# Another written order for the prologue and chunk 0 of fused attention and FFN, with the first loads in the list and a few stages on VectorE

## The chip, the cores and the metric

One core of one Trainium2 chip runs the kernel. The metric is the device time of one launch in microseconds (us). Before the change the median of three runs is 906.14 us (904.85 to 907.07).

## The reference

For each of 8 batches and 8 heads, q, k, v are 576 x 64. Heads 0 to 3 use a local mask (a row sees itself and the 31 rows before it), heads 4 to 7 a strided one (a row sees earlier rows with the same index modulo 32).

```python
scores = np.where(mask, (q @ k.T) / 8.0, -1e9)
attn = np.exp(scores - scores.max(-1)); attn /= attn.sum(-1) + 1e-9
x = concat_heads(attn @ v)                       # 8 x 576 x 512
xn = (x - mu) / np.sqrt(var + 1e-6) * g_ln       # over the 512 columns
out = x + np.maximum(xn @ w_ch1, 0) @ w_ch2      # 512 -> 2048 -> 512
```

The two weight matrices arrive as 64-bit floats, and the kernel turns them into 32-bit ones itself.

## The kernel before, in words

**Tiling.** Attention works on pairs of heads: pair k = 0, 1, 2, 3 is batch 0 (0 and 2 strided, 1 and 3 local), 4 to 7 batch 1, and so on to 31. The FFN works on 9 chunks of 512 rows, chunk c being batch c's first 512 rows (the ninth takes what is left of all batches). The FFN's hidden width of 2048 is cut into 16 steps f of 128. Every matmul of the FFN is split into a high part (`fp32r`) and a rest, so a step is 8 + 4 matmuls for the first layer and 12 for the second.

**Two programs.** Chunks 1 to 8 run in a loop over c and f; the change leaves it as it is. What comes before, the prologue (pairs 0 to 3, whose result is chunk 0's x) and chunk 0 itself (with the weights' conversion and pairs 4 to 8 between), is issued in the order of a hand-written string, `ORDER`. Each engine runs its instructions strictly in that order, and waits by semaphore for what it reads or overwrites. There is no planner at run time: `one(op, k, i, buf)` (L842) carries out one word `op:k:i:buf` of the string.

**The words**, with engine and what they do for pair k:
- `T:k:i` PE, 24 small matmuls that transpose the rows of q (i=0) or k (i=1); `c` ACT, copies that out of PSUM.
- `S` PE, the scores (48 or 80 matmuls); `mask`, `max` DVE; `sub` POOL, minus the row maximum; `exp` ACT.
- `PP` PE, transposes the probabilities; `pt` ACT, copies them; `V` PE, times v; `den`, `xo` DVE, divides by the row sum.
- `X` PE, transposes the result; `xh` ACT and `xl` DVE, its high part and rest, which the first layer reads; `st` stores the result.
- `r`, `v` SP, loads of q and k (8 DMAs) and v for later pairs; `vs` POOL, a shifted copy of v; `tp` DVE, transposes `r`'s tile.

For weight step f: `W` SP, two loads of 512 KB (`w_load`, L221); `sc` ACT, `low` DVE or `lowA` ACT, `mg` and `sg` DVE, which assemble 32-bit floats (i=0 first layer, i=1 second); `byg` POOL, times g; `add` POOL, two adds; `cm` PE, the column mean; `cen` DVE, subtracts it; `hi` ACT and `lo` POOL, high part and rest. Then `F` and `H` PE, the first layer with the high part and the rest (8 and 4 matmuls; for step 0 the last pair's 2 come as `Fb`), `hh` ACT and `hl` DVE after the ReLU, `G` PE, the second layer (12 matmuls).

**What sets the order around the change.** `buf` picks one of three PSUM rooms (`ps_a`, `ps_o[0]`, `ps_o[1]`); a new tile there waits until the old one has been read. The two `ps_o` rooms become the second layer's accumulators at `G:0`. `sc` has a single PSUM buffer (`ps_r`), freed by `sg`. Before `ORDER` starts, lines 802 to 815 issue all loads of batch 0: pair 0's q and k as halves on the SP and ACT queues, q of pairs 1 to 3 on SP's, k on ACT's, then g, then v of the four pairs, all on SP. The first `W` of the list comes behind them on the same queue:

```python
for p in first:
    p.load_v(once=True)
```

Of the kernel before, what the change touches and what calls it, by code (L numbers as in the profile page):

```python
# [32 lines left out]
add:4 hh:2 sg:4:1 st:4 hl:2 sc:5:0 X:4::0 lo:3:0 F:3 mg:5:0 xh:4 r:6 lo:3:1 lowA:5:1 xl:4 H:3
sg:5:0 cm:4::0 hh:3 G:2 cen:4 byg:5 sc:5:1 hl:3 lowA:6:1 v:5 add:5 mg:5:1 hi:4:0 sg:5:1 lowA:6:0
lo:4:0 F:4 max:5 sc:6:0 lowA:7:0 mg:6:0 sub:5 lowA:7:1 cm:5::0 sg:6:0 H:4 cen:5 W:8 sc:6:1 byg:6
G:3 hh:4 mg:6:1 add:6 hi:4:1 hl:4 hi:5:0 sg:6:1 lo:5:0 cm:6::0 sc:7:0 F:5 cen:6 W:9 exp:5 lo:4:1
mg:7:0 hi:5:1 sg:7:0 H:5 tp:6 byg:7 sc:7:1 PP:5::0 lowA:8:0 G:4 add:7 st:0 hh:5 hi:6:0 hl:5 lo:5:1
pt:5 r:7 mg:7:1 hi:6:1 S:6::0 lo:6:0 sg:7:1 lowA:9:0 lowA:8:1 F:6 mask:6 sc:8:0 max:6 cm:7::0
mg:8:0 sg:8:0 sub:6 H:6 st:3 G:5 hh:6 cen:7 byg:8 st:2 hl:6 hi:7:0 lo:6:1 tp:7 sc:8:1 hi:7:1
V:5::0 add:8 lowA:9:1 r:8 F:7 mg:8:1 sg:8:1 lo:7:0 den:5 sc:9:0 xo:5 H:7 mg:9:0 sg:9:0 cm:8::0  # L40
hh:7 G:6 exp:6 byg:9 hl:7 W:10 sc:9:1 cen:8 add:9 mg:9:1 hi:8:0 PP:6::0 hi:8:1 sg:9:1 lo:8:0 F:8
tp:8 pt:6 W:11 lo:7:1 hi:9:1 cm:9::0 H:8 lo:8:1 sc:10:0 cen:9 lowA:10:0 G:7 lowA:10:1 mg:10:0 W:12
hi:9:0 sg:10:0 hh:8 byg:10 sc:10:1 hl:8 S:8::0 lowA:11:0 lo:9:0 mg:10:1 F:9 lowA:11:1 sg:10:1 v:6
add:10 mask:8 sc:11:0 H:9 mg:11:0 lo:9:1 lowA:12:1 sg:11:0 cm:10::0 G:8 hh:9 cen:10 byg:11 W:13
sc:11:1 hi:10:0 mg:11:1 hi:10:1 lo:10:0 hl:9 lowA:12:0 S:7::0 sg:11:1 add:11 sc:12:0 F:10 mask:7
W:14 lo:10:1 mg:12:0 cm:11::0 sg:12:0 H:10 max:7 sc:12:1 byg:12 G:9 hh:10 cen:11 st:5 add:12
mg:12:1 hi:11:0 hl:10 lowA:13:1 W:15 lo:11:0 sg:12:1 hi:11:1 cm:12::0 F:11 max:8 sc:13:0 lowA:13:0
cen:12 H:11 mg:13:0 hi:12:0 v:7 sg:13:0 lo:12:0 X:5::0 hh:11 G:10 xh:5 lo:11:1 sc:13:1 xl:5
lowA:14:1 hl:11 sub:7 hi:12:1 mg:13:1 V:6::0 lowA:14:0 r:9 byg:13 F:12 sg:13:1 den:6 add:13 xo:6
sc:14:0 H:12 lo:12:1 lowA:15:0 mg:14:0 exp:7 cm:13::0 sg:14:0 G:11 hi:13:1 cen:13 byg:14 xr:0  # L50
hh:12 sc:14:1 hl:12 lo:13:1 hi:13:0 mg:14:1 X:6::0 lo:13:0 sg:14:1 F:13 xh:6 add:14 xr:1 sc:15:0
xl:6 H:13 sub:8 mg:15:0 cm:14::0 hh:13 G:12 cen:14 xr:2 sg:15:0 hi:14:0 hl:13 byg:15 xs:0 PP:7::0
lo:14:0 F:14 pt:7 tp:9 st:6 lowA:15:1 add:15 sc:15:1 H:14 r:10 cm:15::0 hh:14 G:13 cen:15 exp:8
hl:14 hi:14:1 mg:15:1 hi:15:0 sg:15:1 lo:15:0 V:7::0 hi:15:1 xr:3 F:15 lo:15:1 den:7 xo:7 lo:14:1
xs:2 X:7::0 v:8 H:15 G:14 hh:15 xh:7 hl:15 xl:7 v:9 tp:10 PP:8::0 pt:8 xs:3 st:7 r:11 xs:1
# [9 lines left out]
def kernel(  # L65
# [737 lines left out]
    for p in first:  # L803
        if p.k in BY_DVE:
            p.load_qk(early.tile([P, 2 * S], F32, name=f"raw{p.id}"))
        elif p.k == 0:
            for i in range(2):
                p.load_rows(i, nc.sync, slice(0, 1))
                p.load_rows(i, nc.scalar, slice(1, 2))
        else:  # L810
            p.load_rows(0, nc.sync)
            p.load_rows(1, nc.scalar)
    nc.sync.dma_start(gcol, g_ln.rearrange("(c p) -> p c", p=P))
    for p in first:
        p.load_v(once=True)

# [211 lines left out]
```

## Time and profile before

| | |
|---|---|
| median of 3 runs | 906.14 us (904.85 to 907.07) |
| the profiled execution | span 907.3 us from the first to the last instruction; the page gives no other time for it |
| PE, matmuls | 884.9 us busy, 98% of the span, 7606 matmuls |
| DVE, ACT, POOL busy | 435.4, 199.7, 147.9 us |
| mean granted TensorE clock | 0.992 |
| F:1, the first layer's second step, starts | at 54.70 us |
| chunk 1 starts (F of its step 0 at 152.55 us, its first G at 162.74 us) | chunks 1 to 8 fill the rest |

The times of the rows are microseconds from the first instruction. A busy time counts an engine's instructions, not its waits. The idle time in brackets behind a row is what the engine spent waiting right before that instruction, and whose end released it; "issue" is a wait for nothing that the profile shows. On PE a row is a run of matmuls; PEld are the weight loads that go with them, one for each. SPq and ACTq are the instructions that issue DMAs.

### The profile page before, as it was taken

How to read it: one execution, taken by the hardware profiler on the slowest of the kernel's cores; microseconds unless marked ns; L12 is line 12 of the kernel's file. 1: busy time of each engine (PE TensorE's matmuls, PEld its weight loads, DVE VectorE, ACT ScalarE, POOL GpSimd, SP SyncE). 2: the span in 40 equal slices, each digit the busy share in tenths (PEclk: the TensorE clock that was granted, in tenths of full speed). 3: DMA queues.
4: the chain of work that ended last, by engine and by line, in shares of the span. 5: the costliest groups of instructions: out<-in, count | busy, mean ns of one | idle time of the engine just before them, and what ended most of it. 6: DMA issues, size and time to landing. Idle time of an engine off the chain costs nothing.

```text
span 907.3 us, 18531 instructions
## 1 busy us (share of the span) xinstructions
PE 884.9 (98%) x7606; PEld 728.8 (80%) x7606; DVE 435.4 (48%) x864; ACT 199.7 (22%) x326; POOL 147.9 (16%) x186
## 2 busy tenths in 40 slices
...
GB/s 166 226 257 179 247 196 114 147 111 119 134 142 109 102 137 120 124 91 141 109 134 93 135 104 141 100 127 124 116 85 91 49 128 0 1 1 93 0 1 47
DMA packets 339621, 102.98 MB, mean 114 GB/s; under 512 B 276944, under 2 KB 331344, under 8 KB 339536
## 3 DMA queue, kind: packets, MB, share of 16 engines
...
q8 instruction: 60, 0.98, 0.5%
q14 instruction: 25, 0.20, 0.1%
...
## 4 chain that ended last, share of the span: by engine, by line
PE 93%; DMA 2%; DVE 1%; issue 1%; SPq 1%; POOL 1%; ACT 0%; DVEq 0%; POOLq 0%; ACTq 0%
PE po L775 42%; PE ph L748 28%; PE ph L755 14%; PE m L515 2%; PE m L445 2%; DMA s<-in_moe_w_ch_dram 1%; PE t L371 1%; PE s L445 1%; DMA rows<-in_q_dram 1%; PE av L515 1%; SPq L351 1%; PE cm L281 1%; PE px L636 0%; PE pp L501 0%; POOL r L270 0%
## 5 line engine op out<-in xcount | busy, mean ns | idle before, releaser
L775 PE MATMUL po<-w,hh 128*128 128x512 f32 x1152 | 359.2, 393 | 0.0
L765 DVE SCALAR_TENSOR_TENSOR hl<-ph,hh 128x512 fp32r<-128x512 f32 x144 | 99.3, 690 | 367.0 <-ACT hh L760 367.0
L775 PEld LDWEIGHTS po<-w,hh 128*128 128x128 f32 x1152 | 213.4, 188 | 44.8
L748 PE MATMUL ph<-xh,w 128*128 128x512 f32 x576 | 226.0, 392 | 1.4 <-ACT w L294 1.2
L775 PE MATMUL po<-w,hl 128*128 128x512 f32 x576 | 224.5, 390 | 0.0
L748 PE MATMUL ph<-xl,w 128*128 128x512 f32 x576 | 224.5, 390 | 0.0
L760 ACT ACTIVATE hh<-ph 128x512 fp32r<-128x512 f32 x144 | 86.1, 598 | 483.7 <-PE ph L755 469.0
L755 PE MATMUL ph<-xh,w 128*128 128x512 f32 x576 | 155.3, 392 | 0.0
L748 PEld LDWEIGHTS ph<-xh,w 128*128 128x128 f32 x576 | 108.3, 188 | 24.1 <-ACT w L294 1.4
L775 PEld LDWEIGHTS po<-w,hl 128*128 128x128 f32 x576 | 108.1, 188 | 23.1
L755 PEld LDWEIGHTS ph<-xh,w 128*128 128x128 f32 x576 | 108.2, 189 | 22.5 <-POOL w L298 0.2
L748 PEld LDWEIGHTS ph<-xl,w 128*128 128x128 f32 x576 | 108.3, 188 | 22.0
L491 POOL TENSOR_TENSOR sm<-sm,mx 128x648 f32<-128x648 f32 (+1 forms) x32 | 40.6, 1269 | 440.4 <-DVE mx L486 440.4
L723 POOL TENSOR_TENSOR rs<-rs,mhalf 128x1 f32<-128x1 f32 x36 | 19.7, 548 | 286.5 <-DVE rs L722 286.5
L497 ACT ACTIVATE sm<-sm 128x648 f32<-128x648 f32 (+1 forms) x32 | 23.8, 742 | 104.3 <-POOL sm L491 104.3
L298 POOL TENSOR_TENSOR w<-r,w 128x512 fp32r<-128x512 f32 x32 | 41.1, 1297 | 7.3 <-ACT w L294 6.9
L687 DVE TENSOR_TENSOR xl<-xo,xh 128x512 fp32r<-128x512 f32 x24 | 16.6, 692 | 38.8 <-ACT xh L686 38.8
L686 ACT ACTIVATE xh<-xo 128x512 fp32r<-128x512 f32 x24 | 15.2, 632 | 62.0 <-DMA pd<-sm 18.2
L486 DVE TENSOR_REDUCE mx<-sm 128x12 f32<-128x648 f32 (+1 forms) x32 | 26.3, 822 | 2.1
L565 DVE TENSOR_TENSOR xo<-m,den 64x64 f32<-64x64 f32 (+3 forms) x120 | 27.1, 289 | 0.0
L781 DVE SCALAR_TENSOR_TENSOR x<-po,rs,x 128x512 f32<-128x512 f32 x36 | 24.5, 737 | 2.0 <-PE po L775 1.8
L718 DVE BATCH_NORM_STATS2 st<-x 128x6 f32<-128x512 f32 x36 | 24.3, 674 | 0.0
...
## 6 DMA issues: line engine op xcount, KB each, us to landing
...
```

The source lines that it names most:

```text
L298: nc.gpsimd.tensor_tensor(out=t[:, 1], in0=self.w[i], in1=t[:, 0].bitcast(F32), op=ALU.subtract)
L445: nc.tensor.matmul(o, lhsT, rhs, start=True, stop=True, tile_position=(64 * h, pos))
L486: nc.vector.reduce_max(mx[:, :, 0:nt], sm, axis=AX.X)
L491: nc.gpsimd.tensor_tensor(out=sm, in0=sm, in1=mx[:, :, 0:nt].unsqueeze(3).broadcast_to([P, 2, nt, sm.shape[3]]), op=ALU.subtract)
L515: nc.tensor.matmul(at(h, t)[m * j:m * (j + 1)], self.p_cols(rows, t, j), self.v[rows, n, 0:w], start=True, stop=True, tile_position=(64 * ...
L565: nc.vector.tensor_tensor(out=xo[r, t0:t1, h0:h1].rearrange("p t h d -> p h t d"), in0=av, in1=den[r, h0:h1, t0:t1].unsqueeze(3).broadcast_to(
L748: nc.tensor.matmul(ph, w1h[:, cc], x[:, cc, :], start=(new and n == 0 and i == 0), stop=False)
L755: nc.tensor.matmul(ph, w1l[:, cc], xt[c][0][:, cc, :], start=False, stop=(cc == NCC - 1))
L760: nc.scalar.activation(out=hh, in_=ph, func=AF.Relu)
L765: nc.vector.scalar_tensor_tensor(out=hl, in0=ph, scalar=0.0, in1=hh.bitcast(F32), op0=ALU.max, op1=ALU.subtract)
L775: nc.tensor.matmul(po[i], hx[:, cs], w, start=(f == 0 and n == 0), stop=(f == NFC - 1 and n == 2))
L781: nc.vector.scalar_tensor_tensor(out=x, in0=po[i], scalar=rs, in1=x, op0=ALU.mult, op1=ALU.add)
```

## The change

The loads of batch 0 become words of the list: `R:k:i` loads the rows of q or k, `g` loads g, and `v:0` to `v:3` load v. All of k but pair 0's second half and pair 1 now goes on SP's queue. `W:0` stands ahead of `R:2:0` and all `v`; `r:4` ahead of `v:1`, and `W:1` behind `v:1`. The list is another one throughout: both are given here up to `G:0`. A word that ends in `D` runs its stage on DVE (`subD:0`, `bygD:14`, `addD:14`, `loD:13:0`, `addD:15`, `loD:15:0`, all POOL before). Step 1's `low` goes to ACT (`lowA:1:0`, `lowA:1:1`), `low:7:1` and `low:15:0` to DVE. The parameters `eng` and `copy` are handed down for that, `BY_DVE` and `ONCE` go, and 2 is written as `CC`; the arithmetic stays.

```diff
 ORDER = """
-T:0:0:0 T:0:1:1 c:0:0: c:0:1: T:1:0:2 S:0::0 c:1:0: T:1:1:2 mask:0 max:0 T:2:1:0 c:1:1: sub:0
-S:1::1 c:2:1: exp:0 T:2:0:2 mask:1 max:1 PP:0::0 c:2:0: T:3:0:1 sub:1 pt:0 c:3:0: V:0::2 exp:1
-vs:1 S:2::0 den:0 xo:0 PP:1::1 mask:2 X:0::2 pt:1 max:2 W:0 T:3:1:0 xh:0 sub:2 V:1::1 xl:0 c:3:1:
-S:3::2 den:1 r:4 xo:1 low:0:0 sc:0:0 low:0:1 exp:2 mg:0:0 mask:3 PP:2::1 X:1::0 pt:2 sg:0:0 W:1
-max:3 xh:1 V:2::2 sc:0:1 xl:1 sub:3 tp:4 byg:0 exp:3 W:2 PP:3::0 add:0 den:2 S:4::1 pt:3 mg:0:1
-vs:3 xo:2 cm:0::0 low:1:0 X:2::2 W:3 mask:4 sg:0:1 V:3::1 xh:2 max:4 sc:1:0 cen:0 sub:4 xl:2 r:5
-hi:0:0 lowA:2:0 mg:1:0 hi:0:1 lo:0:0 F:0 exp:4 den:3 sg:1:0 lowA:3:0 lo:0:1 xo:3 sc:1:1 low:1:1
-byg:1 X:3::1 mg:1:1 v:4 sg:1:1 add:1 PP:4::2 xh:3 sc:2:0 xl:3 cm:1::0 mg:2:0 Fb:0 pt:4 lowA:3:1
-W:4 cen:1 H:0 lowA:2:1 sg:2:0 hi:1:0 tp:5 byg:2 V:4::0 hh:0 sc:2:1 add:2 hl:0 S:5::1 hi:1:1 st:1
-mg:2:1 lo:1:0 cm:2::2 sg:2:1 F:1 W:5 mask:5 sc:3:0 lo:1:1 hi:2:1 cen:2 H:1 mg:3:0 hi:2:0 G:0
...
+R:0:0 T:0:0:1 c:0:0: R:0:1 R:1:1 T:0:1:0 T:1:1:1 c:0:1: c:1:1: S:0::0 R:1:0 R:2:1 mask:0 T:1:0:1
+c:1:0: T:2:1:0 max:0 W:0 subD:0 sc:0:0 exp:0 S:1::1 low:0:0 c:2:1: PP:0::2 mg:0:0 sg:0:0 mask:1
+R:2:0 T:2:0:0 pt:0 v:0 R:3:0 V:0::2 max:1 sc:0:1 low:0:1 g:0 mg:0:1 sub:1 den:0 xo:0 sg:0:1 c:2:0:
+S:2::0 X:0::2 mask:2 exp:1 byg:0 add:0 R:3:1 hi:0:1 lo:0:1 T:3:1:1 xh:0 c:3:1: r:4 T:3:0:0 max:2 v:1
+c:3:0: xl:0 sub:2 exp:2 cm:0::1 cen:0 hi:0:0 PP:1::2 tp:4 S:3::1 pt:1 mask:3 lo:0:0 max:3 W:1
+lowA:1:0 PP:2::2 vs:1 S:4::1 sc:1:0 sub:3 pt:2 v:3 mg:1:0 vs:3 lowA:1:1 mask:4 sg:1:0 V:1::0 exp:3
+PP:3::2 sc:1:1 max:4 v:2 W:2 byg:1 den:1 mg:1:1 pt:3 V:2::1 sub:4 lowA:2:0 r:5 xo:1 X:1::2 den:2
+xh:1 add:1 sg:1:1 W:3 sc:2:0 hi:1:1 xo:2 xl:1 V:3::0 den:3 v:4 X:2::1 lo:1:1 cm:1::2 xh:2 lowA:2:1
+mg:2:0 xo:3 sg:2:0 X:3::0 sc:2:1 byg:2 xl:2 W:4 F:0 cen:1 exp:4 mg:2:1 xh:3 hi:1:0 add:2 cm:2::2
+xl:3 PP:4::1 lowA:3:0 W:7 sg:2:1 tp:5 sc:3:0 lowA:3:1 lo:1:0 Fb:0 H:0 S:5::0 pt:4 mg:3:0 sg:3:0 hh:0
+st:2 hl:0 V:4::1 hi:2:1 cen:2 sc:3:1 byg:3 add:3 mg:3:1 den:4 F:1 W:5 cm:3::2 W:6 hi:2:0 lowA:4:0
+lowA:4:1 lo:2:0 mask:5 xo:4 W:8 lowA:7:0 H:1 cen:3 sg:3:1 hh:1 sc:4:0 X:4::0 hi:3:0 low:7:1 lo:2:1
+hl:1 mg:4:0 sg:4:0 xh:4 G:0 sc:4:1 F:2 H:2 lo:3:0 max:5 hi:3:1 byg:4 mg:4:1 G:1 sg:4:1 lowA:5:0
...
 """
...
     def one(op, k, i, buf):
         p = pairs[k]
-        if op == "T":
+        eng, copy = nc.gpsimd, nc.scalar.copy
+        if op.endswith("D"):
+            op, eng, copy = op[0:-1], nc.vector, nc.vector.tensor_copy
+        if op == "R":
+            if k == 0:
+                p.load_rows(i, nc.sync, slice(0, 1))
+                p.load_rows(i, nc.scalar, slice(1, 2))
+            else:
+                p.load_rows(i, nc.scalar if k == 1 and i == 1 else nc.sync)
+        elif op == "g":
+            nc.sync.dma_start(gcol, g_ln.rearrange("(c p) -> p c", p=P))
+        elif op == "T":
...
         elif op == "v":
-            p.load_v(once=ONCE)
+            p.load_v(once=p.b == 0)
```

## Rows read from the trace of the kernel before

**Rows 1.** Busy time by stage: PE, PEld, DVE, ACT, POOL; granted clock, DMA share, GB/s
```profile
23.44:44.27 20.83, 12.88 (x430) 10.79 (x421) 17.33 (x30) 9.47 (x17) 8.17 (x8) 0.92 0.89 233
44.27:54.70 10.43, 8.22 (x154) 6.28 (x155) 9.46 (x18) 8.07 (x14) 7.87 (x10) 0.84 0.77 212
54.70:112.62 57.92, 57.70 (x503) 47.00 (x503) 49.17 (x77) 40.41 (x70) 45.17 (x47) 1.00 0.83 226
112.62:160.02 47.40, 47.35 (x448) 38.31 (x449) 35.66 (x68) 22.13 (x39) 28.34 (x32) 1.00 0.73 155
160.02:907.30 747.28, 741.18 (x5701) 610.59 (x5699) 318.60 (x652) 110.01 (x178) 46.42 (x55) 1.00 0.50 96
```
**Rows 2.** Timeline of PE up to F:1: start, length, line, count [idle before, releaser]
```profile
8.28 1.21 PE L371 MATMUL t<-ident,rows 96*64 96x96 f32 x24 [1.68 <-DMA rows<-in_q_dram]
...
12.52 0.68 PE L445 MATMUL s<-kt_l,qt_l 64*32 64x64 f32 x42
16.28 0.88 PE L445 MATMUL s<-kt_l,qt_l 64*32 64x64 f32 x38 [3.09 <-issue]
17.09 2.19 PE L371 MATMUL t<-ident,rows 96*64 96x96 f32 x24
19.21 1.54 PE L501 MATMUL pp<-ident,sm 128*128 128x128 f32 x6
20.68 1.71 PE L371 MATMUL t<-ident,rows 96*64 96x96 f32 x24
22.32 0.93 PE L515 MATMUL av<-v_s,pt 54*64 54x65 f32 x48
...
28.65 0.76 PE L515 MATMUL av<-v_l,pt 64*32 64x65 f32 x52 [1.27 <-issue]
...
33.03 0.31 PE L445 MATMUL s<-kt_l,qt_l 64*32 64x64 f32 x5 [2.83 <-issue]
...
49.43 0.79 PE L281 MATMUL cm<-bsum,mean 128*128 128x128 f32 x2 [1.24 <-POOL bsum L277]
...
52.63 0.93 PE L515 MATMUL av<-v_s,pt 54*64 54x65 f32 x48
53.49 1.04 PE L445 MATMUL s<-kt_l,qt_l 64*32 64x64 f32 x80
...
54.70 0.47 PE L748 MATMUL ph<-xh,w 128*128 128x512 f32 x1
```
**Rows 3.** DVE's groups between 23.44 and 54.70 us: busy, mean ns, idle before
```profile
L258 DVE SCALAR_TENSOR_TENSOR p<-p,s 128x512 uint32<-128x512 uint32 x6 | 4.1, 688 | 0.2
L264 DVE SCALAR_TENSOR_TENSOR r<-s,p 128x512 uint32<-128x512 uint32 x5 | 3.3, 657 | 0.0
...
L254 DVE TENSOR_SCALAR s<-s 128x512 uint32<-128x512 uint32 x4 | 1.9, 497 | 0.0
...
L565 DVE TENSOR_TENSOR xo<-av,den 128x768 f32<-128x768 f32 x2 | 1.9, 950 | 0.0
...
L473 DVE TENSOR_TENSOR sm<-s,mask_s 128x648 f32<-128x648 f32 x2 | 1.6, 821 | 0.0
...
L765 DVE SCALAR_TENSOR_TENSOR hl<-ph,hh 128x512 fp32r<-128x512 f32 x1 | 0.7, 693 | 0.5 <-ACT hh L760 0.5
```
**Rows 4.** Timeline of DVE, POOL and ACT: pair 0's max, sub, exp, step 0's sc
```profile
11.35 0.83 DVE L486 TENSOR_REDUCE mx<-sm 128x12 f32<-128x648 f32 x1
12.34 1.27 POOL L491 TENSOR_TENSOR sm<-sm,mx 128x648 f32<-128x648 f32 x1 [3.43 <-DVE mx L486]
13.71 0.76 ACT L497 ACTIVATE sm<-sm 128x648 f32<-128x648 f32 x1
...
27.64 0.64 ACT L244 ACTIVATE p<-s 128x512 f32<-128x512 f32 x1
```
**Rows 5.** Busy time in stretches of 2 us, columns as in rows 1
```profile
0.00:2.00 2.00, 0.95 (x4) 0.95 (x5) 0.96 (x11) 0.00 (x0) 1.26 (x10) 1.00 0.07 16
...
10.00:12.00 2.00, 2.00 (x62) 1.86 (x56) 1.48 (x2) 0.65 (x2) 0.00 (x0) 1.00 1.24 213
...
14.00:16.00 2.00, 0.00 (x0) 0.00 (x0) 0.00 (x0) 0.47 (x1) 0.00 (x0) 0.73 0.37 72
...
34.00:36.00 2.00, 1.49 (x54) 1.22 (x52) 1.93 (x5) 1.77 (x3) 0.20 (x1) 1.00 1.04 379
```
**Rows 6.** Timeline of SP's queue: loads of W:0 (first half) and r:4
```profile
20.22 0.49 SPq L224 DMA_DIRECT2D s<-in_moe_w_ch_dram  x1
...
21.39 3.04 SPq L351 DMA_DIRECT2D raw<-in_q_dram  x4
24.47 4.30 SPq L351 DMA_DIRECT2D raw<-in_k_dram  x4
```
**Rows 7.** The page's DMA queues: PE's instructions, packets and MB
```profile
q8 instruction: 60, 0.98, 0.5%
```

More of the change, by code (lines that the diff above doesn't have):

```diff
@@ L33 @@
[L33 to L55, printed above, removed]
-"""
-BY_DVE = ()
@@ new lines @@
+lowA:4:1 lo:2:0 mask:5 xo:4 W:8 lowA:7:0 H:1 cen:3 sg:3:1 hh:1 sc:4:0 X:4::0 hi:3:0 low:7:1 lo:2:1
+hl:1 mg:4:0 sg:4:0 xh:4 G:0 sc:4:1 F:2 H:2 lo:3:0 max:5 hi:3:1 byg:4 mg:4:1 G:1 sg:4:1 lowA:5:0
+lowA:5:1 sc:5:0 xl:4 mg:5:0 hi:4:1 hh:2 add:4 sg:5:0 hl:2 cm:4::0 lo:3:1 sub:5 lowA:6:0 F:3 sc:6:0
+mg:6:0 byg:5 sg:6:0 lowA:6:1 st:1 add:5 st:3 exp:5 cen:4 sc:5:1 cm:5::0 H:3 byg:6 mg:5:1 add:6
+sg:5:1 cen:5 hi:4:0 lowA:8:0 sc:7:0 hh:3 hi:5:1 mg:7:0 sg:7:0 G:2 sc:7:1 hl:3 r:6 cm:6::0 mg:7:1
+lo:4:0 lowA:8:1 sg:7:1 hi:5:0 cen:6 F:4 H:4 sc:8:0 mg:8:0 lo:4:1 hi:6:0 sg:8:0 hh:4 sc:6:1 PP:5::0
@@ new lines @@
+tp:6 mg:6:1 pt:5 G:3 hi:7:1 hl:4 S:6::0 sg:6:1 sc:8:1 hi:6:1 W:9 mask:6 F:5 lo:5:1 v:5 lo:5:0 byg:7
+mg:8:1 lowA:9:0 lowA:9:1 st:0 sg:8:1 lo:6:0 r:7 byg:8 sc:9:0 add:7 cm:7::0 H:5 cen:7 lo:7:1 hh:5
+hi:7:0 max:6 hl:5 mg:9:0 lo:6:1 sub:6 G:4 st:4 add:8 sg:9:0 tp:7 V:5::0 hi:8:1 W:10 exp:6 sc:9:1
+lo:8:1 den:5 xo:5 mg:9:1 F:6 byg:9 sg:9:1 lowA:10:0 cm:8::0 lo:7:0 H:6 sc:10:0 cen:8 mg:10:0
+lowA:10:1 sg:10:0 hi:8:0 hh:6 G:5 hl:6 r:8 W:11 sc:10:1 add:9 byg:10 W:12 PP:6::0 W:14 mg:10:1 W:13
+sg:10:1 st:5 lo:8:0 tp:8 hi:9:1 F:7 pt:6 cm:9::0 hi:10:1 H:7 sc:11:0 cen:9 lowA:11:0 mg:11:0 G:6
```

83 lines of the change are left out of this document (39 added, 44 removed).

## The prediction

> **What bounds the kernel now.** I read the busy time by stage first, then PE's timeline, and then asked what DVE, POOL and SP did where PE stood idle. From F:1 at 54.70 us on, PE is the bound: in the 57.92 us to 112.62 it is busy 57.70, in the next 47.40 it is busy 47.35, and the eight loop chunks behind run at 741.18 of 747.28, which the change leaves alone [rows 1]. An order can't make that part shorter, it can only bring holes into it. So what there is to win lies ahead of F:1. There PE waits: 1.68 us for pair 1's rows, 3.09 us inside pair 1's scores, 1.27 and 2.83 us in V:1 and S:3, 1.24 us for step 1's column sum [rows 2].
>
> Second reading: from den:0, which DVE starts as V:0 ends, to F:1 are 31.3 us (23.44 to 54.70), and in them DVE is busy 17.33 + 9.46 = 26.8 [rows 1]. DVE has no long holes there but 4.5 us of short ones, ACT is at 17.5 and POOL at 16.0. So F:1 comes when DVE has done its list from den:0 on, plus what DVE waits for PE. Both lists have done the same PE work by F:1 (all T, S:0 to 5, PP:0 to 4, V:0 to 4, X:0 to 3, cm:0 to 2, F, Fb and H of step 0), so PE itself saves nothing: the change can only start DVE's list earlier, shorten it, or remove waits.
>
> **Part 1: up to den:0.** The new list opens T:0:0 T:0:1 T:1:1 S:0 T:1:0 T:2:1 S:1. These are the same matmuls that stand before the 3.09 us hole now, in another order: 12 wake-up matmuls, 5 x 24, 48 and 42, so 222. T:1:1 needs pair 1's k, which moves in the same place of ACT's queue as now, beside pair 1's q on SP's; both kinds landed by 8.28 [rows 2]. I therefore keep S:1 ending at 17.1. Behind it now come T (2.1 us to the next start), PP:0 (1.5), T (1.6), V:0 at 22.32; then PP:0, T:2:0, V:0. One T less stands ahead, worth 1.6 to 2.1 us by the two rows; I take 1.9, so den:0 at 21.55.
>
> What must be ready by then, and what it costs if not:
> - subD:0 takes the place of a POOL subtraction of 1.27 us that started 0.16 us after max:0 [rows 4]. On DVE the trace has no such one; the mask add of the same 648 elements takes 0.821 [rows 3]. DVE idles there, exp:0 would end at about 13.9 and PE is in S:1 until 17.1. Worth 0; at 1.27 or more it would still be hidden.
> - sc:0:0 now stands ahead of exp:0 on ACT and waits for W:0's first half. Ahead of it in the queues are 1.44 MB of rows (four halves and three whole loads); at 213 GB/s from 2 us on (before, 16 GB/s) [rows 5] that ends at 8.8, and 0.52 MB at 379 GB/s [rows 5] at 10.2. For the landing I add 1 us, an estimate from pair 1's rows: 1.15 MB at the same rate make 7.4, and they were there at 8.28 [rows 2]. So 11.2; exp:0 is wanted at 13.0 and hidden until 16.3, which leaves 4 to 5 us of reserve. A worst end: the first read of W:0 in the trace comes 7.4 us after its issue [rows 4, 6], and from an issue near 4 us that is 11.4 as well. Worth 0.
> - v:0 now stands behind W:0 (1.05 MB) and q of pair 2. By the same rates 1.73 MB of rows, W:0 and 0.29 MB of v are in at 2 + 8.1 + 2.8 + 1.4 + 1, 15.3; V:0 wants it at 20.2. In the trace v stood at 72 GB/s in one stretch [rows 5]; at that rate it would take 4.0 for the 1.4 and land at 17.9. Worth 0.
> - r:4 starts on SP when the rows are issued, some 16 us, and its eight DMAs held SP for 7.4 us [rows 6]: landed near 25, wanted by tp:4 at 27. Then v:1, then W:1, issued near 24.5. If it lands in 4 us, lowA:1:0 on ACT (wanted at 28.5) does not wait; if it takes the 7.4 us of W:0, ACT stands 3.4 us with sc:1:0 and pt:2 behind it, and mg:1:0 on DVE behind those. This is the tightest transfer: 0 to 3.4 us. I take 0, since SP's queue holds no other weights by then, and keep the other end.
>
> **Part 2: DVE from den:0 to tp:5.** F:1 stands behind V:4 and S:5 on PE, and S:5 needs tp:5, DVE's last piece. Against the 26.8 us of now: step 0's two `low` go before den:0 and step 1's to ACT (4 x 0.497 = 2.0); mg of step 0 goes before den:0 (2 x 0.688 = 1.4), sg:0:0 too (0.657), but sg:2:1 comes in (0.657); hl:0 moves behind F:1 (0.69) [rows 3]. That is 4.1 less, 22.7 us. ACT, which takes two `lowA` for the two `low`, is busy 17.5 of 31.3 and covers them.
>
> DVE's waits inside are 4.5 us now [rows 1]. The 1.27 and 2.83 us holes make a good part of them, since V:1 and S:3 gave DVE its next work. In the new list S:3 is followed on DVE by tp:4 (2.5 us of transposes) before mask:3 wants it, and V:1 is wanted only after mask:4 and max:4. A hole of 1 to 3 us in either place is covered. Left are xl:0 behind X:0 and xh:0, and short ones, so I take 2.0; the ends are 0 and 4.5.
>
> Sum: tp:5 ends at 21.55 + 22.7 + 2.0 = 46.25; S:5 and V:4 take 1.0 and 0.9 [rows 2], F:1 starts at 48.2. That is 6.5 us earlier.
>
> **Part 3: given back after F:1.** X:4 has moved ahead of G:0. It needs xo:4, which ends 5.6 us after tp:5 on DVE (mg, sg, hl, cen, mg at about 0.69, den 0.4, mask 0.82, xo 0.95), at 51.8, while PE is through F:1, cm:3 and H:1 at about 51.2: 0.6 us. G:0 also needs the two PSUM rooms read, by xo:4 and by cen:3 right behind. From F:2 on the words keep a lead of one to two steps. POOL takes 45.17 of 57.92 us and DVE 49.17 [rows 1], so both have room, and the stages moved to DVE late (bygD:14 to loD:15:0) fall where it is busy 35.66 of 47.40. PE lost 0.27 us in the same part before. I put down 0.4 more, so 1.0 in all. W:11 to W:14 stand behind r:8 on SP; a late landing stops ACT at sc:11:0, but hh:7 behind it has G:6, S:8, F:8 and H:8, over 6 us, before G:7 wants it.
>
> Result: 6.5 - 1.0 = 5.5 us. The profiled execution's span is 907.3, which would become 901.8; it lies 1.16 above the median, so the median goes to 906.14 - 5.5 = 900.6.
>
> **A rule that speaks against it.** PE's instructions come over a queue of their own: 60 packets with 0.98 MB [rows 7], 16.3 KB each, for 15,212 matmuls and weight loads, so one packet holds 127 of such pairs. Counted along PE's timeline, the three holes without a releaser come at matmul 222, 473 and 600, 251 (2 x 126) and 127 apart: they lie at packet ends, and the one at 222 came while the other queues moved 213 GB/s [rows 2, 5]. The Trainium skill (Runtime: NRT & Kernel Launch, Instruction fetch mechanics) says that the next 16 KiB block is fetched while the current one runs and the crossing is mostly hidden; the trace disagrees with 7.2 us of holes. By that rule the new list would gain 3.1 us more. The skill's DMA: Bandwidth & Descriptors (Queues, rings and completion order) has every DMA engine go round its queues by whole packets; by it larger transfers ahead, as W:0's are, would make a fetch later. No row separates the two.
>
> **The rivals.**
> - *The hole in S:1 closes.* The fetch's neighbours change. S:1 then ends at 14.1, PP:0 waits for exp:0, and V:0 comes at about 17.5, behind PP:0, T:2:0 and v:0: 2.7 us more, 898. Against it: by 10 us the queues are as full as now. Chance 0.10.
> - *Half is lost on the way.* W:1 late by 2 us, or DVE's waits stay at 4.5, or the hole grows by 2 to 3 us with W:0 moving: 2.5 less, 903.5 (902.8 to 905). For it: the 7.4 us of the rows. Chance 0.17.
> - *No change that counts.* F:1 comes early, but PE then stands until the step preparation catches up where it always was. By DVE's 49.17 of 57.92 this needs 8.7 us of disorder, and the preparation is itself early. 906; chance 0.07.
> - *Slower: PE waits for column sums.* The new list puts cm:5 ahead of H:3, cm:6 ahead of F:4, two steps ahead of their use. cm waits for sg on DVE, then byg and two adds on POOL; in the trace such a wait cost 1.24 us once [rows 2]. It decides once POOL's second add for a step ends after F of the step two before. At 0.8 us in each of 12 steps it costs 9.6, less the 6.5: 909. Against it: POOL idles 12.7 of 57.92 us. Chance 0.10.
>
> **How the numbers follow.** Forecast 0.56 (898.5 to 902.8), and the rivals as above. A measurement here can tell 0.3%, 2.7 us, from no change, so faster means below 903.4: 0.56 + 0.10 + 0.07 of the half lost, 0.73. Same is the rest of that one and the no-change case, 0.17. Slower 0.10. The range 897.5 to 906.5 leaves out some of the first rival and the slower one.
>
> **What would show it.** Right: the hole of about 3 us in S:1 stays, den:0 near 21.5, DVE nearly without holes from there, tp:5's end near 46 and F:1 near 48, PE full from then on but for a short wait at X:4. Wrong: ACT waiting for weights at sc:0:0 or lowA:1:0, V:0 waiting for v, DVE idle over 4 us between den:0 and F:1, or holes of PE at cm after F:2.

## The result, and the profile after

The changed kernel takes **914.6 us** (median of 4 runs, 911.7 to 915.28) against 906.61 for the kernel before (median of 4, 904.85 to 908.16): ratio **1.0083, 95% interval 1.006 to 1.0105**. It is slower; the forecast was 900.6 (897.5 to 906.5). The profiled execution has a span of 909.9 us and a time of 911.7, so a time is its span and 1.8. Six more runs of it (e0) have a median of 913.85.

Busy time by stage after, cut as in [rows 1]: at den:0, F:0 and F:1, then at the same 112.62 and 160.02 us as there, to the end (columns as there).

```profile
27.31:46.38 19.07, 14.24 (x472) 11.50 (x473) 18.14 (x34) 13.47 (x23) 16.67 (x17) 1.00 0.89 223
46.38:53.39 7.01, 6.20 (x151) 4.75 (x149) 6.97 (x13) 6.43 (x12) 4.19 (x5) 1.00 1.02 276
53.39:112.62 59.23, 57.06 (x500) 45.55 (x496) 53.34 (x85) 44.07 (x77) 50.28 (x53) 1.00 0.97 262
112.62:160.02 47.40, 46.21 (x444) 37.36 (x443) 30.47 (x57) 16.33 (x28) 14.62 (x16) 1.00 0.56 105
160.02:909.90 749.88, 743.89 (x5712) 612.96 (x5711) 321.06 (x660) 109.89 (x178) 46.73 (x55) 1.00 0.49 95
```

Two things differ from before. den:0 starts at 27.31 us instead of 23.44. And behind F:1 PE is no longer full: 2.17 us idle of 59.23 and 1.19 of 47.40, against 0.22 and 0.05. The DMA share there is 0.97 instead of 0.83 [rows 1]: 59.23 us at 262 GB/s are 15.5 MB, 57.92 at 226 were 13.1, so the new list moved 2.4 MB more by then, over two steps' weights.

**The opening.** ACT's timeline of the changed kernel, the DMAs that it issues and its instructions (start, length):

```profile
0.74 0.43 ACTq L360 DMA_DIRECT2D rows<-in_q_dram  x1
...
6.52 1.24 ACT L381 COPY qt_s<-t 128x576 f32<-128x576 f32 x1 [4.03 <-PE t L370]
6.58 3.15 ACTq L360 DMA_DIRECT2D rows<-in_k_dram  x2
15.79 1.24 ACT L381 COPY kt_s<-t 128x576 f32<-128x576 f32 x1 [8.03 <-PE t L370]
```

PE's timeline of the same kernel, for the same time:

```profile
4.02 2.48 PE L370 MATMUL t<-ident,rows 96*64 96x96 f32 x26
13.57 2.18 PE L370 MATMUL t<-ident,rows 96*64 96x96 f32 x22 [7.08 <-DMA rows<-in_k_dram]
16.26 2.19 PE L370 MATMUL t<-ident,rows 96*64 96x96 f32 x24 [0.51 <-DMA rows<-in_k_dram]
```

In the new list `c:0:0`, a copy on ACT, stands ahead of `R:0:1 R:1:1`. The two loads of k on ACT's queue are therefore issued behind a copy that waits for PE's T:0:0: at 6.58 us, where ACT's four k loads went out from 1.21 us on before. SP has by then issued W:0 and is busy with v:0 (4.52 to 13.57 us). PE stands 7.08 us at T:0:1.

**Behind F:1.** PE's waits there that ended with `hl` (PE's timeline of the changed kernel); their sum, 2.5 us, is also on the page's row of L744:

```profile
93.68 0.50 PE L744 MATMUL ph<-xh,w 128*128 128x512 f32 x1 [0.81 <-DVE hl L761]
101.30 0.50 PE L744 MATMUL ph<-xh,w 128*128 128x512 f32 x1 [0.78 <-DVE hl L761]
...
122.93 0.50 PE L744 MATMUL ph<-xh,w 128*128 128x512 f32 x1 [0.69 <-DVE hl L761]
129.82 0.50 PE L744 MATMUL ph<-xh,w 128*128 128x512 f32 x1 [0.23 <-DVE hl L761]
```

ACT's timeline ahead of the first two (L249 is lowA:10:0, L242 sc:11:0, L756 hh):

```profile
89.29 0.68 ACT L249 ACTIVATE s<-s 128x512 uint32<-128x512 uint8 x1 [3.79 <-issue]
...
92.32 0.58 ACT L756 ACTIVATE hh<-ph 128x512 fp32r<-128x512 f32 x1
...
97.98 0.63 ACT L242 ACTIVATE p<-s 128x512 f32<-128x512 f32 x1 [2.30 <-DMA s<-in_moe_w_ch_dram]
...
99.09 0.58 ACT L756 ACTIVATE hh<-ph 128x512 fp32r<-128x512 f32 x1
```

SP's queue in that time: W:10, r:8's eight DMAs, W:11's first half:

```profile
84.11 0.58 SPq L222 DMA_DIRECT2D s<-in_moe_w_ch_dram  x1
84.73 0.92 SPq L225 DMA_DIRECT2D s<-in_moe_w_ch_dram  x1
86.13 2.79 SPq L350 DMA_DIRECT2D raw<-in_q_dram  x4
88.96 4.63 SPq L350 DMA_DIRECT2D raw<-in_k_dram  x4
93.63 0.50 SPq L222 DMA_DIRECT2D s<-in_moe_w_ch_dram  x1
```

Read from the bottom: r:8 holds SP from 86.13 to 93.6 us, W:11 is issued behind it, ACT stands 2.30 us at sc:11:0, `hh` waits behind that on ACT and `hl` behind `hh` on DVE, and the next step's F waits until `hl` has read `ph`, which has one PSUM buffer. The hole at 93.68 us comes the same way from W:10, issued at 84.11 us behind r:7 and st:4. SP's own rows between 54 and 112 us sum to 55.9 us after (64 DMAs), to 38.8 before (61).

One table for all that follows, from the profiles (us). In each kernel the span is F:1, the time from F:1 to chunk 1's first F, and 755, within 0.4: the loop is the same everywhere. (In the profile of before, chunk 1's first F is at 152.31 us; the 152.55 given ahead of the prediction is 0.24 too late.)

| kernel | den:0 | F:1 | F:1 to chunk 1 | span | median, ratio to before |
|---|---|---|---|---|---|
| before | 23.44 | 54.7 | 97.6 | 907.3 | 906.6 |
| before, again | 21.55 | 52.3 | 97.6 | 904.7 | one run, 906.5 |
| after | 27.31 | 53.4 | 101.7 | 909.9 | 914.6, 1.0083 |
| e0, after again | 27.80 | 55.4 | 102.4 | 912.7 | 913.85, 1.008 |
| e1, k first | 21.02 | 49.0 | 102.4 | 906.5 | 911.26, 1.0047 |
| e1 again | 20.03 | 53.9 | 104.3 | 913.1 | one run, 914.9 |
| e2, weights first | 27.34 | 53.7 | 112.0 | 920.7 | 922.54, 1.018 |
| e3, both | 20.33 | 51.0 | 115.3 | 921.3 | 922.53, 1.0168 |
| e4, before's tail | 21.69 | 50.4 | 100.7 | 906.1 | 910.9, 1.0051 |
| e5, no stage on DVE | 28.13 | 54.1 | 101.5 | 911.0 | 913.82, 1.0076 |
| e6, before with W:0 early | 23.71 | 53.9 | 97.6 | 906.4 | 907.37, 1.001 |
| e7, xo:4 early | 19.14 | 51.7 | 99.1 | 905.8 | 906.93, 0.9995 |
| e7 again | 21.34 | 52.6 | 98.9 | 906.6 | one run, 908.45 |
| e8, fill | 28.12 | 59.8 | 104.1 | 918.9 | 920.7, 1.0157 |
| e9, W:3 first | 21.64 | 51.1 | 97.7 | 904.0 | 905.81, 0.9988 |
| e10, W:2 too | 22.87 | 51.5 | 97.7 | 904.5 | 906.29, 0.9991 |

### The profile page after: what moved, and what is told of

The parts are those of the page before. It is cut to its first block, busy times and chain, and to the rows that moved or that the text cites. A ratio compares the mean times of both kernels' runs of the same rounds, so it can differ in the third digit from the quotient of the medians.

```text
span 909.9 us, 18505 instructions
## 1 busy us (share of the span) xinstructions
PE 885.4 (97%) x7606; PEld 727.8 (80%) x7606; DVE 438.6 (48%) x872; ACT 200.1 (22%) x326; POOL 140.6 (15%) x178
## 4 chain that ended last, share of the span: by engine, by line
PE 85%; DMA 6%; SPq 4%; DVE 2%; POOL 2%; issue 1%; ACT 0%; DVEq 0%; POOLq 0%
PE po L771 40%; PE ph L744 26%; PE ph L751 13%; PE m L511 2%; PE m L442 2%; SPq L350 2%; DMA v_s<-in_v_dram 2%; DMA s<-in_moe_w_ch_dram 2%; DMA xdl<-xo 1%; SPq L222 1%; POOL w L296 1%; SPq L225 1%; DMA x<-xds 1%; POOL sm L488 0%; SPq L360 0%
## 5 line engine op out<-in xcount | busy, mean ns | idle before, releaser
L744 PE MATMUL ph<-xh,w 128*128 128x512 f32 x576 | 226.0, 392 | 2.5 <-DVE hl L761 2.5
L744 PE MATMUL ph<-xl,w 128*128 128x512 f32 x576 | 224.5, 390 | 0.0
L756 ACT ACTIVATE hh<-ph 128x512 fp32r<-128x512 f32 x144 | 85.9, 596 | 477.9 <-PE ph L751 434.4
L744 PEld LDWEIGHTS ph<-xh,w 128*128 128x128 f32 x576 | 108.1, 188 | 25.5 <-DVE hl L761 3.3
L771 PEld LDWEIGHTS po<-w,hl 128*128 128x128 f32 x576 | 108.1, 188 | 22.9
L744 PEld LDWEIGHTS ph<-xl,w 128*128 128x128 f32 x576 | 108.2, 188 | 22.3 <-DVE xl L663 0.3
L488 POOL TENSOR_TENSOR sm<-sm,mx 128x640 f32<-128x640 f32 (+1 forms) x31 | 39.4, 1270 | 447.1 <-DVE mx L483 447.1
L296 POOL TENSOR_TENSOR w<-r,w 128x512 fp32r<-128x512 f32 x30 | 38.7, 1298 | 6.8 <-ACT w L292 6.7
```

The source lines that it names most:

```text
L296: eng.tensor_tensor(out=t[:, 1], in0=self.w[i], in1=t[:, 0].bitcast(F32), op=ALU.subtract)
L488: eng.tensor_tensor(out=sm, in0=sm, in1=mx[:, :, 0:nt].unsqueeze(3).broadcast_to([P, 2, nt, sm.shape[3]]), op=ALU.subtract)
L744: nc.tensor.matmul(ph, w1h[:, cc], x[:, cc, :], start=(new and n == 0 and i == 0), stop=False)
L756: nc.scalar.activation(out=hh, in_=ph, func=AF.Relu)
L771: nc.tensor.matmul(po[i], hx[:, cs], w, start=(f == 0 and n == 0), stop=(f == NFC - 1 and n == 2))
```

## The experiments

Theory A puts the loss into the opening, at the k loads. B puts it behind F:1, at the weights that come late on SP's queue; B' at the order of chunk 0's words as a whole. C, the rival, is the low clock that can follow PE's idle time. The prediction's own rival had PE wait for POOL's sums.

**e0**, the changed kernel unchanged, and **before_again**.

> The changed kernel once more, for a second profile. Theory A (opening): the k loads on ACT's queue stand behind c:0:0, so PE again idles about 7 us before T:0:1 and S:0 starts near 18. Theory C (clock): the changed kernel's first profile kept the full clock throughout (mean 0.999) while its other runs had 0.988 to 0.991 and took 2.4 to 3.6 us more; if the low clock after the long idle is a cost of its own, a profile with clock near 0.99 shows half clock somewhere between 14 and 50 us and a time near 914 to 915. Without it 911 to 912.

> The kernel before once more, for a second profile beside the first (span 907.3, which lies above most of its runs). Expected: span 903 to 907, F:1 between 52 and 55 us, and holes of PE without a releaser at the same matmuls (222, 473, 600) but of other lengths; 97.6 to 98.0 us from F:1 to chunk 1's first F, as in the first profile.

e0: 913.85 us, ratio 1.008 (1.0064 to 1.0095). Its profile has the same wait at T:0:1, 8.28 us, and the granted clock falls to 0.50, which is 1.2 GHz. Busy time in stretches of e0, granted clock in the third column from the end:

```profile
10.00:20.00 10.00, 5.55 (x94) 5.06 (x94) 0.00 (x0) 1.88 (x2) 0.00 (x0) 0.50 1.14 169
20.00:22.00 2.00, 2.00 (x34) 1.90 (x31) 1.52 (x2) 0.00 (x0) 0.00 (x0) 0.50 0.63 66
```

PE's timeline of e0, T:1:1:

```profile
16.63 2.19 PE L370 MATMUL t<-ident,rows 96*64 96x96 f32 x24 [0.40 <-DMA rows<-in_k_dram]
```

The first profile shows a granted clock of 1.00 all along, but its matmuls don't bear that out: T:1:1's 24 took the same 2.19 us in it, at 16.26, and 1.21 us in e1, where the clock there is 1.00. From the end of PE's wait at T:0:1 to den:0 the two profiles take 13.74 and 13.75 us. So they don't differ by the clock in the opening, and the expectation's comparison of their mean clocks falls. F:1 comes 2.0 us later in e0. k landed 0.5 us later, and the holes without a releaser between den:0 and F:1 are 1.7 us longer: 0.81 us in S:3 and 2.30 in V:1, against 1.01 in V:1 and 0.41 in V:3.

The profile of before that the prediction used turns out to be a late one: again, S:1's hole is 1.63 us, not 3.09, and F:1 stands at 52.3. PE's timeline of before_again:

```profile
16.39 0.64 PE L445 MATMUL s<-kt_l,qt_l 64*32 64x64 f32 x38 [1.63 <-issue]
...
30.01 0.43 PE L445 MATMUL s<-kt_l,qt_l 64*32 64x64 f32 x5 [2.57 <-issue]
```

**e1**, the k loads ahead of the copy, nothing else.

```diff
-R:0:0 T:0:0:1 c:0:0: R:0:1 R:1:1 T:0:1:0
+R:0:0 R:0:1 R:1:1 T:0:0:1 c:0:0: T:0:1:0
```

> One move: R:0:1 and R:1:1 ahead of T:0:0 and c:0:0, so ACT issues its k loads near 1 us again; all else as changed. Theory A: the 7 us hole goes, S:0 starts near 9.5 to 11, F:1 near 48 to 49, and the time falls by about 5 us, to 909. Rival B (chunk 0's end is set by late weights and DVE's order, not by the opening): F:1 comes early, but PE waits more behind it and the time falls by less than 1.5 us, 913 to 914.

911.26 us, 1.0047 (1.003 to 1.0064): 2.6 us back in the median. PE no longer waits at T:0:1, and 1.31 us at T:1:1; den:0 is at 21.02 and F:1 at 49.0, nearly as forecast for the change. PE's timeline of e1, T:1:1, and DVE's, the end of tp:5:

```profile
8.39 1.21 PE L370 MATMUL t<-ident,rows 96*64 96x96 f32 x24 [1.31 <-DMA rows<-in_k_dram]
...
46.08 0.76 DVE L413 STREAM_TRANSPOSE kt_l<-raw 128x576 f32<-128x576 f32 x1
```

A is right for its place; what it is worth fell short of the expected 5 us.

**e2**, W:10 ahead of r:7, W:11 and W:12 ahead of st:4 and r:8, and **e3**, that and e1's edit.

```diff
-lo:6:0 r:7
+lo:6:0 W:10 r:7
...
-G:4 st:4 add:8 sg:9:0 tp:7 V:5::0 hi:8:1 W:10 exp:6
+G:4 W:11 W:12 st:4 add:8 sg:9:0 tp:7 V:5::0 hi:8:1 exp:6
...
-r:8 W:11 sc:10:1 add:9 byg:10 W:12 PP:6::0
+r:8 sc:10:1 add:9 byg:10 PP:6::0
```

> SP's order alone: W:10 ahead of r:7, W:11 and W:12 ahead of st:4 and r:8; the opening as changed. Theory B: ACT's waits of 3.8 and 2.3 us for the weights of steps 10 and 11 go, with them PE's waits for hl at F near 93 and 101 us, 2 to 3 us in all, so 911 to 912; F:1 stays near 53.4. Rival D (DVE is simply too full in chunk 0, whatever the weights do): the waits for hl move to other steps and the time stays within 1 us, 913.6 to 915.6.

> Both edits. If A and B are separate costs they add: 7 to 8 us less than the changed kernel, 906 to 908. If B's stalls exist only because the opening is late, or the early opening meets weights that are even later, the sum is less than the larger of the two by itself plus 1 us: 908 to 910. The blind forecast of 900.6 would need another 6 us.

922.54 (1.0158 to 1.0201) and 922.53 (1.0147 to 1.0189): both far above their expectations. The holes for `hl` near 93 and 101 us are gone, but st:4 was issued behind the weights, at 90.63 us instead of 83.06. DVE's timeline of e2:

```profile
99.49 0.82 DVE L560 TENSOR_TENSOR xo<-av,den 128x640 f32<-128x640 f32 x1 [7.87 <-DMA xds<-xo]
```

PE's timeline of e2:

```profile
100.46 0.76 PE L278 MATMUL cm<-bsum,mean 128*128 128x128 f32 x2 [12.35 <-DVE xo L560]
```

xo:5 writes the one buffer that st:4 still reads. DVE stood 7.87 us with everything of the next steps queued behind, and PE 12.35 (14.15 in e3). SP's order sets this stretch as B has it, but its weights can't simply go first.

**e4**, the new list as in e1 up to F:1, from there before's list without the words already done. **e5**, the changed kernel with the six `D` words on POOL. **e6**, the kernel before with step 0's weights ahead of v.

```diff
-subD:0 ... bygD:14 ... addD:14 ... loD:13:0 ... addD:15 ... loD:15:0
+sub:0 ... byg:14 ... add:14 ... lo:13:0 ... add:15 ... lo:15:0
```

```diff
+    w_load(0)
     for p in first:
         p.load_v(once=True)
...
-pt:1 max:2 W:0 T:3:1:0
+pt:1 max:2 T:3:1:0
```

> The new list with its k loads first (as in e1_k_first) up to F:1, and behind F:1 the order of the kernel before, less the words already done (all on the engines of before; SP's loads in the order of before too). Theory B' (the loss behind F:1 lies in the new list's order of chunk 0: loads of weights behind those of q and k, stores and x loads late, DVE and ACT standing in line behind them, so that hh or hl comes late for PE): F:1 near 49 as in e1_k_first, holes of PE behind it under 1 us instead of 4, and the time 3 to 5 us under e1_k_first's 911.3, at 906 to 908. If the old order meets the earlier start without loss it may come to 902 to 905. Rival (an earlier F:1 always gives back what it gained, since the preparation of the weights is what sets the pace in chunk 0): the holes come back elsewhere, 910 to 912.

> The changed kernel with the six stages marked D (subD:0, bygD:14, addD:14, loD:13:0, addD:15, loD:15:0) back on POOL; the order as changed. Theory B': they matter little, since DVE is late by waiting and not by these 3 us: within 1 us of the changed kernel's 914. Rival D (DVE too full): hl near 123 and 130 us comes earlier and the time falls by 1 to 2 us, 912 to 913; if instead POOL is then late with steps 14 and 15, it grows by 1 to 2 us.

> The kernel before with one edit: step 0's weights are loaded ahead of v, behind g. If the weights' 1 MB ahead of v costs by itself, V:0 (22.3 us) waits for v and the time grows by 1 to 3 us, 908 to 910. If v lands in time, as the prediction had it, nothing changes, 906 to 907; a hole at PE's instructions may move by up to 2 us either way.

e5 is 913.82 (1.0061 to 1.0091), level with e0: no effect of the stages on DVE shows either way. e6 is 907.37, ratio 1.001 (0.9996 to 1.0025): no cost of W:0 ahead of v shows. e4 is 910.9 (1.0033 to 1.0069), 3 to 5 us over its expectation. Its profile is of an execution of 907.86 us and has one hole behind F:1, made by the splice (the new list has V:4 in the room that G:0 wants, before's has xo:4 only behind F:2). PE's timeline of e4:

```profile
56.34 0.70 PE L770 MATMUL po<-w,hh 128*128 128x512 f32 x2 [2.97 <-DVE xo L560]
```

Without it, F:1 to chunk 1 would be 97.8 us, 0.2 from before. That speaks for B'; e7 tests it.

**e7**, e4 with xo:4 right behind F:1, twice; **e1_again**; and **e8**, the changed kernel with 12 matmul calls (24 matmuls) that nothing reads, in the 7 to 8 us in which PE waits.

```diff
-F:1 W:5 mask:5 H:1 ... F:2 sg:3:1 xo:4
+F:1 xo:4 W:5 mask:5 H:1 ... F:2 sg:3:1
```

```diff
-R:0:0 T:0:0:1 c:0:0: R:0:1
+R:0:0 T:0:0:1 c:0:0: K:0:12 R:0:1
...
+        if op == "K":
+            fill = ps_h.tile([P, CH], F32, tag="h", name="fill")
+            for _ in range(i):
+                nc.tensor.matmul(fill[:, 0:P], mean, mean, start=True, stop=True)
```

> The list of e4 with xo:4 right behind F:1 instead of behind F:2, nothing else. Theory B' (what is lost behind F:1 is lost by the order of chunk 0's words): the one hole that e4 had behind F:1, 2.97 us at G:0 for xo:4, goes or shrinks below 1 us; chunk 1's first F comes near 148.5 us (97.5 to 98.5 behind F:1, F:1 near 50); the median falls by 2 to 3 from e4's 910.9 to about 908, and to 905 or below if the clock is no further cost. Rival C' (the early opening leaves PE at the low clock ahead of F:1, and this is on the path): the hole goes too, but F:1 moves with the clock from run to run, between 49 and 53, and the median stays at 908 to 911, level with or above before's 906.7.

> The kernel of e7 once more, for a second profile: by C' the two profiles differ by where F:1 stands and by the granted clock ahead of it, and are alike (within 0.5 us) from F:1 on; by the rival they differ behind F:1.

> The kernel of e1 once more, for a second profile, since its first profiled execution (908.26) was the fastest of its six. Theory C': an execution of 910 to 912 shows F:1 later than 49.0 by most of the difference, beside a lower granted clock ahead of F:1, and 102 us from F:1 to chunk 1 as in the first. Rival B: F:1 stays near 49, and the holes behind it, at hl and the loads, are longer. Third: the difference lies behind 160 us, in the loop.

> The changed kernel with 12 idle matmuls (mean times mean, never read) behind T:0:0, some 5.9 us in the 7 to 8 us in which PE waits for pair 0's second half and pair 1's k; nothing that another engine does is touched. Theory C (the low clock that follows this idle time costs 2 to 3 us in most runs): the granted clock stays at 1.00 to 20 us, F:1 comes at 53.4 as in the first profile of the changed kernel instead of 55.4, and the median falls from 913.9 to 911.5, with a mean clock of 0.995 or more. Rival (the clock ahead of F:1 is not on the path, DVE and the loads are): median 913.5 to 914.5, F:1 as before the edit.

e7 is 906.93 against 907.12, ratio 0.9995 (0.998 to 1.001): the hole is gone and 4.3 us of e1's 911.26 with it. B' holds for the holes: PE is idle 0.15 of the 99.1 us behind F:1, against 4.1 of e1's 102.4. The other 1.5 us over before's 97.6 are the clock's, with the same 808 matmuls in that time. PE had waited at V:4, 1.03 us for pt:4 and 0.78 for v:4, and the granted clock was 0.50 behind that, to 55 us. Busy time in a stretch of e7, and PE's timeline there, a matmul of F:1 that takes 0.63 us instead of 0.39:

```profile
50.00:60.00 10.00, 9.22 (x77) 7.49 (x77) 6.33 (x12) 4.75 (x9) 3.79 (x5) 0.83 1.04 343
...
53.43 0.63 PE L743 MATMUL ph<-xh,w 128*128 128x512 f32 x1
```

And F:1 is at 51.7 and 52.6, not near 50. e1_again shows why. SP's queue in e1, r:5 and then the first half of W:3:

```profile
32.05 3.33 SPq L350 DMA_DIRECT2D raw<-in_q_dram  x4
35.43 3.28 SPq L350 DMA_DIRECT2D raw<-in_k_dram  x4
38.75 0.50 SPq L222 DMA_DIRECT2D s<-in_moe_w_ch_dram  x1
```

The same of e1_again:

```profile
33.57 4.37 SPq L350 DMA_DIRECT2D raw<-in_q_dram  x4
37.98 5.16 SPq L350 DMA_DIRECT2D raw<-in_k_dram  x4
43.18 0.50 SPq L222 DMA_DIRECT2D s<-in_moe_w_ch_dram  x1
```

ACT's timeline of e1_again behind that (step 3's weights, then pt:4):

```profile
47.95 0.69 ACT L249 ACTIVATE s<-s 128x512 uint32<-128x512 uint8 x1 [2.28 <-DMA s<-in_moe_w_ch_dram]
...
50.06 0.67 ACT L249 ACTIVATE s<-s 128x512 uint32<-128x512 uint8 x1 [0.89 <-DMA s<-in_moe_w_ch_dram]
50.63 0.78 ACT L503 COPY pt<-pp 128x768 f32<-128x768 f32 x1
```

PE's timeline of e1_again, V:4 and F:1:

```profile
51.47 0.41 PE L511 MATMUL av<-v_s,pt 54*64 54x65 f32 x2 [2.14 <-ACT pt L503]
52.36 1.57 PE L511 MATMUL av<-v_s,pt 54*64 54x65 f32 x46 [0.48 <-DMA v_s<-in_v_dram]
53.86 0.79 PE L744 MATMUL ph<-xh,w 128*128 128x512 f32 x1
```

The same eight DMAs held SP for 6.7 us in one execution and 9.6 in the other. W:3 is issued 4.4 us later, ACT waits for it with pt:4 behind, V:4 waits 2.14 us for pt:4 and 0.48 for v:4, and F:1 comes 4.9 us later; 1.3 of these stand already at S:5. Of the 6.6 us between the two spans 4.9 lie there and 1.9 behind F:1, where the clock was low as in e7:

```profile
50.00:60.00 10.00, 8.06 (x70) 6.65 (x71) 6.28 (x13) 6.22 (x11) 4.75 (x5) 0.66 0.95 293
```

e8 went against C's expectation: 920.7, 6.8 above e0. k landed no earlier, PE still waited 4.65 us and the clock was 0.63 from 10 to 20 us, so it says nothing on the clock's cost in the opening. The 24 matmuls moved the holes instead. PE's timeline of e8:

```profile
59.50 0.33 PE L510 MATMUL av<-v_s,pt 54*64 54x65 f32 x3 [3.70 <-issue]
```

Counted along PE this hole lies at matmul 979. In the changed kernel V:4 ends with matmul 958, so 979 falls 21 behind it; 24 matmuls put ahead bring the same place into V:4, and F:1 comes 4.4 us later than in e0. The clock is 0.50 behind this hole too, and F:1 to chunk 1 takes 1.6 us longer than in e0.

**e9**, e7 with W:3 ahead of r:5, and **e10**, that with W:2 right behind W:1.

```diff
-lowA:2:0 r:5 xo:1 X:1::2 den:2 xh:1 add:1 sg:1:1 W:3 sc:2:0
+lowA:2:0 W:3 r:5 xo:1 X:1::2 den:2 xh:1 add:1 sg:1:1 sc:2:0
```

> The list of e7 with W:3 ahead of r:5 on SP's queue, nothing else. Theory S (the new opening is bound by SP's queue: r:5's eight DMAs held it for 8 to 9.5 us and W:3 stood behind them, so ACT waits 2 to 3 us for step 3's weights with pt:4 queued behind): W:3 is issued near 34 us instead of 42 to 43, ACT's waits for weights between 44 and 50 us (2.0 and 4.1 us in e7's two profiles) go, pt:4's copy no longer holds V:4, F:1 comes at 49.5 to 50.5 instead of 51.7 and 52.6, and the median falls by 1.5 to 2.5 from e7's 906.9 to about 905. Rival C' (the low clock ahead of F:1 decides): the waits go, but F:1 stays at 51 to 53 and the median within 0.7 of 906.9. Third: r:5 is now the late one, tp:5 waits on DVE for it and S:5 with it, 1 to 2 us, and the median stays or rises.

> e9 with W:2 right behind W:1 as well, ahead of the v loads of pairs 3 and 2. Theory S: ACT's wait for step 2's weights near 38 us (2.6, 0.8 and 1.9 us in the profiles of e7 and e1) goes too; the v loads are issued about 1 us later, V:2 and V:3 want them at 33 to 38 us; together F:1 at 49 to 50 and the median 904 to 905. Rival: v is now late, PE waits at V:2 for a microsecond or two and pt:3, xo:2 and all behind come later, and the median is at or above e9's.

SP's queue of e9, W:3's first half and that of r:5:

```profile
34.10 0.43 SPq L221 DMA_DIRECT2D s<-in_moe_w_ch_dram  x1
...
36.61 3.92 SPq L349 DMA_DIRECT2D raw<-in_q_dram  x4
```

ACT's timeline of e9, step 3's last piece and pt:4:

```profile
46.94 0.66 ACT L248 ACTIVATE s<-s 128x512 uint32<-128x512 uint8 x1
47.51 0.78 ACT L502 COPY pt<-pp 128x768 f32<-128x768 f32 x1
```

PE's timeline of e9, V:4 and F:1:

```profile
50.29 0.92 PE L510 MATMUL av<-v_s,pt 54*64 54x65 f32 x46 [1.17 <-DMA v_s<-in_v_dram]
51.14 0.50 PE L743 MATMUL ph<-xh,w 128*128 128x512 f32 x1
```

W:3 goes out at 34.10 instead of 42.01, and ACT no longer waits at step 3's weights: pt:4 is copied at 47.51 us, 48.88 in e7. V:4 now waits 1.17 us for v:4, which stands behind r:5, so F:1 is at 51.1 and not at the 49.5 to 50.5 expected. Of the 1.8 us between the spans of e7 and e9, 1.4 lie behind F:1, where e9 keeps the clock:

```profile
50.00:60.00 10.00, 9.71 (x86) 8.17 (x87) 5.76 (x12) 3.63 (x7) 4.87 (x7) 1.00 1.03 339
```

The median is 905.81 against 907.23 for before, ratio 0.9988 (0.9975 to 1.0001). That is the lowest of all lists, 1.4 us under before, and the interval just touches no change. e10 is 906.29 (0.9977 to 1.0006), not better than e9: step 2's wait at ACT is gone, but den:0 came 1.2 us later in its profile, behind a hole of 2.04 us in S:1 that e9 lacks and that lies ahead of the words moved. No list here beats the kernel before by more than the measurement can tell.

In ratios to before, then, the loss is made up: 1.008 to 1.0047 (k loads), to 0.9995 (order behind F:1), to 0.9988 (W:3). The last step alone is not clear of the noise: the intervals of e7 and e9 overlap.

## Why the prediction was wrong

- **The step that failed first** is in part 1: "T:1:1 needs pair 1's k, which moves in the same place of ACT's queue as now". The words show the k loads behind `c:0:0`, and ACT issues DMAs in its instruction order. So den:0 came at 27.31 us and not 21.55. With the loads moved it came at 19.1 to 22.9 in eight profiles (e1, e3, e4, e7, e9, e10), 21.02 in e1's first: the rest of that sum was about right.
- **Costs put at nothing.** subD:0, sc:0:0 with W:0, and v:0 were worth 0: no wait of ACT or PE for them in the profile after, nor in e1 with the earlier opening; e5 and e6 agree.
- **The weights' landing.** Called the tightest transfer, "0 to 3.4 us. I take 0", and only for r:4 and W:1. The queue's time was not summed. r:5 ahead of W:3 is the later and dearer case: ACT waited 2.28 + 0.89 us for W:3 in e1_again. This is the forecast's rival "Half is lost on the way" with another weight, and it shows only where the opening is early.
- **Part 2** held where nothing else was late. From den:0 to the end of tp:5 DVE is busy 23.1 us in after, e1 and e9 (forecast 22.7). In e1's first profile it waits 2.7 us (forecast 2.0), tp:5 ends at 46.84, S:5 follows at 46.98 and F:1 at 48.98: 28.0 us behind den:0, forecast 26.7. The profile after took 26.1 us, but den:0 was late and the loads had 6 us more to land. In e1_again and e7 the stretch takes 31.3 to 33.8 us: DVE waits more on the way, and V:4 then waits 1.8 to 3.7 us for pt:4 and v:4, so there the loads end last and not DVE's list.
- **Part 3** was mis-sized: 1.0 us, measured 4.1 (first profiles) to 4.8 (the second ones). PE's idle time behind F:1 grew by 3.1 us (0.28 to 3.35) in the first; the other 1.0 is spread over its matmuls, and no run here shows why. The place was named: "a late landing stops ACT at sc:11:0, but hh:7 behind it has G:6, S:8, F:8 and H:8, over 6 us, before G:7 wants it". ACT did stop there, 2.30 us. The cover was counted to the wrong reader: the next F wants `ph` back from `hl`, long before G wants `hh`.
- **The base.** The forecast set 907.3 against the median with an offset of 1.16. But time is span and 1.8, so that execution was 909.1, some 2.5 above the median, with F:1 at 54.70 where a second profile has 52.3. Of the 6.5 us forecast at F:1, 2.4 were that execution's own lateness, 1.5 of them in S:1's hole (3.09 against 1.63). The forecast's F:1 at 48.2, 98.6 behind it, 755 and 1.8 make 903.6 and not 900.6.
- **The rivals.** "Slower" came true by another way: PE's waits at cm behind F:1 are 0.30 and 0.28 us in the profile after and end with DVE, not POOL. "The hole in S:1 closes" happened too: S:1 ran through behind the 7 us wait, and that won nothing.
- **The rule on instruction fetch** (the Trainium skill, Runtime: NRT & Kernel Launch, Instruction fetch mechanics, the crossing mostly hidden) is not borne out in the first 60 us, and is behind them. Each of the 16 profiles has two to four holes without a releaser of over 0.1 us up to there, at the matmul numbers 221, 347, 474, 601, 727 or 979 within one, e8 with its 24 more matmuls too. Of the some 50 packets behind, one has such a hole (0.12 us, e10). The hole in S:1 was 0.68 to 3.65 us where it came; e3, e7's first profile and e9 have k early and none. The forecast put 213 GB/s beside the hole at 222. That is the stretch from 10 to 12 us; the hole lies from 13.19 to 16.28, and 14 to 16 has 72 [rows 5].

What stays open: how much the clock costs ahead of F:1. In the profile after, T:0:1, T:1:1 and S:0 took 5.9 us behind the wait, at e1's pace they take 3.2, so 2.7 us is an upper end for the opening, an estimate from these rows. Why the typical run of e1 and e4 lies 3 us above their first profiles is shown for one execution of e1 (e1_again), not for the others, and why the same DMAs hold SP for different times is not shown at all.
